# Low halves of the gate and value weights by an adding transfer from GpSimd instead of a VectorE subtraction

## The chip, the core and the metric

The kernel runs on one core of a Trainium2 chip. The metric is the device time of one execution in microseconds, lower is better. Five engines of the core work beside each other, each through its own instructions in their order: TensorE (PE, with its weight loads PEld), VectorE (DVE), ScalarE (ACT), GpSimd (POOL) and SyncE (SP), which here only issues transfers. They wait for each other through semaphores.

## What is computed

```python
def reference(**kwargs):
    attn_out = _attn_ref(**attn_kwargs)                     # q, k, v: (4, 8, 576, 64)
    x = np.ascontiguousarray(attn_out.transpose(0, 2, 1, 3)).reshape(B * S, H * D)
    x = _moe_ref(x=x, **moe_kwargs)                         # 512 -> 1536 -> 512
    return _moe2_ref(x=x, **moe2_kwargs)                    # 512 -> 2048 -> 512

def _attn_ref(q, k, v):
    scores = scale * np.matmul(q, k.transpose(0, 1, 3, 2))
    mask = (rel >= 0) & (rel < 128)
    scores = np.where(mask, scores + bias[None], -1000000000.0)
    attn = softmax of scores along the keys
    return np.matmul(attn, v)

def _moe_ref(x, w_gate, w_val, w_out):
    g = x @ w_gate
    silu = g * (1.0 / (1.0 + np.exp(-g)))
    val = x @ w_val
    return silu * val @ w_out
```

The weights reach the chip as 64-bit floats. Windowed attention with a linear bias makes 2304 tokens of 512 numbers; a gated layer (gate and value weights, then an output weight) and a second layer follow.

## The kernel before, in words

**Split operands.** Matmuls of the two layers run on operands rounded to a shorter 32-bit format (fp32r). To keep accuracy every operand is a pair, a high half (the rounded value) and a low half (the value minus its high half), and a product is three matmuls: high by high, high by low, low by high (`hid`, `proj`, `products`).

**Five chunks of tokens.** The 2304 tokens go through attention and the first layer in chunks of 512, 384, 512, 512 and 384. While PE does the first layer of one chunk, the attention of the next is woven between its groups. Chunk 0 of the first layer is the place that the change touches: a group is one block i of 128 hidden columns (i = 0 to 11). Its gate product is `g()` (12 matmuls of 512 columns), its value product `v()` (12 more), and its part of the output product `o()` (12). The text calls them g5, v5, o5 and so on. Each needs the weight tile w5, a tile of two halves, `h[:, 0]` and `h[:, 1]`.

**Weights made on the way.** `stage_w1` has SP load a raw tile of 64-bit numbers (`wst`, 1 MB). `convert` makes a 32-bit float of it in five steps: one on ACT (L421, into `cg`), four on DVE (L426, L433, L438, L444). L433 is the first that writes the 32-bit tile `cw`, L444 the last. `halves` then has ACT round it into the high half (`hi_act`, L121) and DVE subtract that from it into the low half (`lo_dve`, L124). The same five steps and `halves` make the tiles of the output weight (`conv_ring`, tile `ring`); these are also written to DRAM from `cw`.

**What sets the order.** PE's order is written out by hand. The conversions are a queue of small steps (`bg`) which `pump` takes from between the groups of PE's order, in chunk 0 so that the steps of w(i+2) are handed out about while group i is handed out. On the other engines the scheduler of the framework orders the instructions by its own estimate of when they are ready, so each of DVE, ACT and POOL has a fixed order when the program runs, and an instruction that waits holds up what is behind it on its engine.

**Buffers.** `cw` has two buffers, which the conversions of w, those of `ring` and, at the end of a chunk, the evacuation share. Weight tiles and raw tiles share a pool of 12 (`wp`). The PSUM banks of the scores, the transposed probabilities, the attention output and the gate and value products rotate through four (`rot`): a bank comes free when DVE or ACT has read it.

**POOL** only clears small tiles (`memset`, L204) and masks the transposed probabilities (`affine_select`, L268 and L272, six to a head in chunk 1); the attention output `o_ps` waits for the masks. All transfers are issued by SP.

Of the kernel before, what the change touches and what calls it, by code (L numbers as in the profile page):

```python
# [9 lines left out]
F32 = mybir.dt.float32  # L10
# [5 lines left out]
AF = mybir.ActivationFunctionType  # L16
ALU = mybir.AluOpType
# [75 lines left out]
def body(ctx: ExitStack, tc: tile.TileContext, qT, kT, vP, w1, w1o, w2, cst, yT):  # L93
    nc = tc.nc
# [25 lines left out]
    def hi_act(out, in_):  # L120
        return nc.scalar.activation(out=out, in_=in_, func=AF.Copy)  # L121

    def lo_dve(out, in_, hi):
        return nc.vector.tensor_tensor(out=out, in0=in_, in1=hi.bitcast(F32), op=ALU.subtract)  # L124
# [282 lines left out]
    def steps(key, fs, front=False):  # L407
        if front:
            bg.extendleft([(key if f is fs[-1] else None, f) for f in fs][::-1])
            return  # L410
        for f in fs[:-1]:
            bg.append((None, f))
        bg.append((key, fs[-1]))

    def convert(raw, st):
        words = raw.rearrange("p (n t) -> p n t", t=2)
        top16 = raw.bitcast(BF16).rearrange("p (n t) -> p n t", t=4)[:, :, 3]

        def f1():
            st["g"] = bpool["a"].tile([128, 1024], BF16, tag="cg", name="cg", bufs=2)  # L420
            nc.scalar.activation(out=st["g"], in_=top16, func=AF.Prelu, scale=2.0 ** -112, alpha=-(2.0 ** 32))  # L421

        def f2():
            st["p"] = bpool["a"].tile([128, 1024], BF16, tag="cp", name="cp", bufs=1)
            g, p = st["g"].bitcast(I32), st["p"].bitcast(I32)
            nc.vector.tensor_scalar(  # L426
                out=p, in0=g, scalar1=3, scalar2=-0x007F0080, op0=ALU.logical_shift_left, op1=ALU.bitwise_and
            )

        def f3():  # L430
            st["w"] = hp_.tile([128, 1024], F32, tag="cw", name="cw")
            a = st["w"].bitcast(I32)
            nc.vector.tensor_scalar(  # L433
                out=a, in0=words[:, :, 1], scalar1=0xFFFFF, scalar2=0x100000, op0=ALU.bitwise_and, op1=ALU.bitwise_or
            )

        def f4():
            nc.vector.scalar_tensor_tensor(  # L438
                out=st["w"], in0=words[:, :, 0].bitcast(U32), scalar=2.0 ** -32, in1=st["w"].bitcast(I32),
                op0=ALU.mult, op1=ALU.add,  # L440
            )

        def f5():
            nc.vector.scalar_tensor_tensor(  # L444
                out=st["w"], in0=st["w"], scalar=2.0 ** -20, in1=st["p"], op0=ALU.mult, op1=ALU.mult
            )

        return [f1, f2, f3, f4, f5]

    def halves(st, alloc, put):  # L450
        def f1():
            st["h"] = alloc()
            hi_act(st["h"][:, 0], st["w"])

        def f2():
            lo_dve(st["h"][:, 1], st["w"], st["h"][:, 0])
            put(st["h"])

        return [f1, f2]

    def w_tile():
        return wp.tile([128, 2, 1024], F32R, tag="w", name="w")

# [3 lines left out]
    stage = {}  # L467

    def stage_w1(i):
        stage[i] = wp.tile([128, 2048], I32, tag="w", name="wst")  # L470
        nc.sync.dma_start(out=stage[i], in_=w1[i].bitcast(I32))
# [5 lines left out]
    def conv_w1(i):  # L477
        st = {}

        def put(w):  # L480
            wt[i] = w
            stage.pop(i)
            if i + 4 < NF1:
                stage_w1(i + 4)

        steps(("w", i), convert(stage[i], st) + halves(st, w_tile, put))

    def conv_ring(r):
        st = {}
# [442 lines left out]
    with tc.manual_schedule(engines={mybir.EngineType.PE}):  # L932
# [28 lines left out]
        while at < lasts[0]:  # L961
            pieces.popleft()[2]()
            at += 1
            if at == 1:
                conv_w1(0)
                conv_ring(0)
                conv_w1(1)
                nst = len(bg)
                stage_w1(2)
                stage_w1(3)  # L970
            f = (at / lasts[0] - CFG["conv_a"]) / (CFG["conv_b"] - CFG["conv_a"])
            while bg and nst - len(bg) < f * nst:
                pump(1)
        carry = []
        behind += [last_of["act"], last_of["x", 2]]
        for ci, p in enumerate(plansA):
# [33 lines left out]
            for gi, (kind, i, f) in enumerate(groups):  # L1010
                if ci == 0 and kind == "gv" and gi % 3 == 0:
                    if i + 2 < NF1:
                        conv_w1(i + 2)
                    if i == 0:
                        conv_ring(1)
                f()
                if ci or not win:
                    pump(CFG["pump_g"])
                elif gi % 3 == 0:
                    due = max(1, -(-len(bg) // 4))  # L1020
                if not ci:
                    pump(due)
                while win and (spent * ng < (gi + 1) * total or gi == len(groups) - 1):
                    _, cost, e = win.popleft()
                    e()
                    spent += cost
                    pump(CFG["pump_p"] if ci else due)
# [76 lines left out]
```

## Time and profile before

| | |
|---|---|
| device time, median of 3 runs | 962.4 us (958.83 to 965.27) |
| device time of the profiled execution | 964.91 us |
| its span in the trace | 963.2 us |
| PE busy | 927.9 us (96%) |
| DVE busy | 699.3 us (73%) |
| ACT busy | 526.1 us (55%) |
| POOL busy | 213.8 us (22%) |

All rows come from one profiled execution; times in them are microseconds from the start of the span. Busy time is the time in which an engine worked on instructions. In a timeline a row stands for one or more like instructions, xN is their number, and the bracket at its end is the idle time of the engine ahead of it with the instruction that ended it. PEclk is the clock that TensorE was granted, as a share of 2.4 GHz, so that 0.50 is the lower level of 1.2 GHz.

### The profile page before, as it was taken

What the parts mean: (1) busy time and instruction counts of PE and PEld (TensorE: products, weight loads), DVE (VectorE), ACT (ScalarE), POOL (GpSimd) and SP (SyncE); (2) the same over time, 40 slices, a digit from 0 to 9 for tenths busy, and PEclk for the clock granted to TensorE, in tenths of its full rate; (3) what the DMA queues carried; (4) which work ended last, traced back from release to release, by engine and by line L of the source; (5) the groups of instructions that cost most, each with busy time, mean ns of one, the idle gap of its engine ahead of it and who ended that gap; (6) DMA issues with size and microseconds to landing.
All of it is one profiled execution on the core that took longest, in us unless ns stands there. A gap on an engine that the chain in (4) does not pass through costs nothing. (4 is left out here: it accounts for less than half of the span.)

```text
span 963.2 us, 14607 instructions
## 1 busy us (share of the span) xinstructions
PE 927.9 (96%) x5040; PEld 831.0 (86%) x5040; DVE 699.3 (73%) x1341; ACT 526.1 (55%) x1135; POOL 213.8 (22%) x332
## 2 busy tenths in 40 slices
PE   6999989999999999998999998899999999999998
PEld 4757777899988888886878998889999999999998
DVE  6789998688767855477434668778876888777673
ACT  6757676666575764445433445555544645454442
POOL 0217422101211122001113334552012320122000
PEclk9979999999999999999999999999999999999999
DMA  8736536377537632276306993624784257830375
GB/s 304 284 110 249 176 103 195 92 243 264 161 86 246 220 115 94 73 233 212 113 1 215 378 325 109 251 66 156 259 296 141 66 180 250 309 116 21 95 259 193
DMA packets 76921, 174.86 MB, mean 182 GB/s; under 512 B 9136, under 2 KB 52528, under 8 KB 67120
## 3 DMA queue, kind: packets, MB, share of 16 engines
q1 hardware_dynamic: 76848, 173.94, 54.3%
q8 instruction: 40, 0.66, 0.3%
q14 instruction: 33, 0.27, 0.1%
HBM read 138.25 MB, written 35.65 MB: 181 GB/s over the span
## 5 line engine op out<-in xcount | busy, mean ns | idle before, releaser
L114 PE MATMUL g_ps<-xt,w 128*128 128x512 f32 (+1 forms) x1440 | 320.6, 376 | 1.3 <-ACT xt L121 0.7
L114 PEld LDWEIGHTS g_ps<-xt,w 128*128 128x128 f32 x1440 | 260.0, 190 | 38.9 <-issue 2.4
L114 PE MATMUL bk<-xs,win 128*128 128x384 f32 x1008 | 179.0, 336 | 8.0 <-DVE G L699 6.0
L114 PEld LDWEIGHTS bk<-xs,win 128*128 128x128 f32 x1008 | 174.4, 188 | 12.2 <-DVE G L699 9.6
L114 PE MATMUL bk<-op,wout 128*128 128x384 f32 x1008 | 175.6, 334 | 0.4 <-DMA wout<-w2o 0.4
L114 PEld LDWEIGHTS bk<-op,wout 128*128 128x128 f32 x1008 | 174.8, 188 | 0.7 <-issue 0.7
L114 PE MATMUL acc<-hh,ring 128*128 128x512 f32 (+1 forms) x480 | 150.2, 376 | 2.3 <-DVE ring L124 1.6
L268 POOL TENSOR_SCALAR_AFFINE_SELECT PT<-PT 128x256 f32<-128x256 f32 (+4 forms) x80 | 55.5, 710 | 247.5 <-ACT PT L265 247.4
L121 ACT ACTIVATE op<-G 128x768 fp32r<-128x768 f32 x84 | 70.7, 846 | 65.6 <-PE bk L114 63.1
L114 PEld LDWEIGHTS acc<-hh,ring 128*128 128x128 f32 x480 | 89.8, 190 | 16.0 <-DVE ring L124 2.3
L124 DVE TENSOR_TENSOR op<-G,op 128x768 fp32r<-128x768 f32 x84 | 80.1, 960 | 26.9 <-ACT op L121 26.4
L795 POOL TENSOR_TENSOR t<-w 128x256 f32<-128x256 f32 x48 | 44.4, 945 | 224.6 <-DVE win L124 205.8
L114 PE MATMUL acc<-hl,ring 128*128 128x512 f32 (+1 forms) x240 | 89.2, 372 | 0.8 <-DVE hl L124 0.8
L237 ACT ACTIVATE Pt<-Pt,sm 128x128 f32<-128x128 f32 (+1 forms) x160 | 62.4, 392 | 20.5 <-DVE sm L233 20.1
L634 DVE SCALAR_TENSOR_TENSOR t<-t,g_ps 128x512 f32<-128x512 f32 (+1 forms) x60 | 37.6, 627 | 37.6 <-ACT t L633 37.5
L633 ACT ACTIVATE t<-g_ps 128x512 f32<-128x512 f32 (+1 forms) x60 | 32.8, 546 | 53.1 <-PE g_ps L114 52.6
L699 DVE TENSOR_TENSOR G<-u,bk 128x384 f32<-128x384 f32 x72 | 38.9, 552 | 31.4 <-PE bk L114 29.3
L1048 ACT ACTIVATE G<-G 128x384 f32<-128x384 f32 x72 | 36.9, 519 | 44.2 <-DVE G L699 44.2
L642 DVE SCALAR_TENSOR_TENSOR t<-t,g_ps 128x512 f32<-128x512 f32 (+1 forms) x60 | 37.8, 630 | 28.4 <-PE g_ps L114 27.4
L121 ACT ACTIVATE hh<-t 128x512 fp32r<-128x512 f32 (+1 forms) x60 | 35.0, 583 | 40.5 <-DVE t L642 40.4
L252 ACT ACTIVATE Pt<-Pt,sm 128x128 f32<-128x128 f32 (+1 forms) x144 | 46.3, 391 | 12.2 <-DVE sm L248 12.1
L114 PEld LDWEIGHTS acc<-hl,ring 128*128 128x128 f32 x240 | 45.5, 190 | 6.3 <-DVE hl L124 1.1
(78 smaller groups left out, 1241.0 us busy)
## 6 DMA issues: line engine op xcount, KB each, us to landing
wout<-w2o SPq DMA_DIRECT2D x42, 1024.0 KB, 5.8
wraw<-w SPq DMA_DIRECT2D x16, 1024.0 KB, 5.9
w2o<-chl SPq DMA_DIRECT2D x16, 896.0 KB, 8.3
wst<-w SPq DMA_DIRECT2D x12, 1024.0 KB, 7.2
cw<-w1od SPq DMA_DIRECT2D x24, 512.0 KB, 4.0
w<-w2d SPq DMA_DIRECT2D x24, 512.0 KB, 3.4
w2d<-cw SPq DMA_DIRECT2D x16, 512.0 KB, 4.3
wraw<-w1o SPq DMA_DIRECT2D x6, 1024.0 KB, 5.1
```

Of the source, the lines that this page charges most:

```text
L114: nc.tensor.matmul(out=out, lhsT=lhsT, rhs=rhs, start=start, stop=stop, skip_group_check=True)
L121: return nc.scalar.activation(out=out, in_=in_, func=AF.Copy)
L124: return nc.vector.tensor_tensor(out=out, in0=in_, in1=hi.bitcast(F32), op=ALU.subtract)
L237: nc.scalar.activation(out=Pt[:q.qn], in_=Pt[:q.qn], func=AF.Exp, scale=-1.0, bias=sm[:q.qn, i:i + 1], accum_out=sm[:q.qn, 8 + i:9 + i],)
L252: nc.scalar.activation(out=pt, in_=pt, func=AF.Copy, scale=r)
L268: nc.gpsimd.affine_select(out=here, in_=prev, pattern=[[0, m], [1, n]], compare_op=ALU.is_ge, fill=0.0, base=0, channel_multiplier=-1,)
L633: tanhs.append(nc.scalar.activation(out=t[:, :n], in_=st["g"][:, :n], func=AF.Tanh, scale=0.5))
L634: nc.vector.scalar_tensor_tensor(out=t[:, :n], in0=t[:, :n], scalar=1.0, in1=st["g"][:, :n], op0=ALU.add, op1=ALU.mult)
L642: nc.vector.scalar_tensor_tensor(out=t[:, :n], in0=t[:, :n], scalar=0.5, in1=vps[:, :n], op0=ALU.mult, op1=ALU.mult)
L699: nc.vector.tensor_tensor(out=out, in0=a, in1=b, op=op)
L795: nc.gpsimd.tensor_tensor(out=x[:, o], in0=a, in1=b, op=ALU.subtract)
L1048: nc.scalar.activation(out=out, in_=in_, func=AF.Mish)
```

## The change

For the weight tiles 2 to 11 the two steps of `halves` are replaced by those of `fold`. ACT rounds the 32-bit tile into the high half as before. Then ACT writes the negated high half into the place of the low half, and a transfer issued by GpSimd adds the 32-bit tile onto it. The tiles 0 and 1, all `ring` tiles and the second layer's weights keep the subtraction on DVE.

```diff
@@ -458,6 +458,19 @@
+    def fold(st, put):
+        def f1():
+            st["h"] = w_tile()
+            hi_act(st["h"][:, 0], st["w"])
+
+        def f2():
+            h = st["h"]
+            nc.scalar.activation(out=h[:, 1], in_=h[:, 0].bitcast(F32), func=AF.Copy, scale=-1.0)
+            nc.gpsimd.dma_start(out=h[:, 1].bitcast(F32), in_=st["w"], accum_op=ALU.add)
+            put(h)
+
+        return [f1, f2]
+
@@ -483,7 +496,7 @@
-        steps(("w", i), convert(stage[i], st) + halves(st, w_tile, put))
+        steps(("w", i), convert(stage[i], st) + (fold(st, put) if i > 1 else halves(st, w_tile, put)))
```

The 13 new lines move every later line: L633 and L642 of before are L646 and L655 after. PE's order stays as it is. On the other engines the scheduler sets a new order, for the stretch in which chunk 0 of the first layer runs and, in a few places, near the end of the chunks. Three places of it follow. The number behind a name tells one buffer's use from the next; in brackets stands which engines or transfers the instruction waits for (DMAHW: a transfer issued by SP, DMASW: one issued by GpSimd).

On DVE, before the change, the stretch in which the first output-weight tile of the woven part (`cw_825`) and w5 (`cw_895`) begin to be converted. `t_820` is the gate of group 3 (L634), `hl_749` the low half of group 2's hidden block.

```order
L124 TENSOR_TENSOR w_788<-cw_771,w_788 128x1024 [waits DMAHW3_49,Activation_49]
L438 SCALAR_TENSOR_TENSOR cw_825<-wraw_643,cw_825 128x1024 [waits DVE_49]
L248 RECIPROCAL sm_664<-sm_664 128x4 [waits DVE_49]
L124 TENSOR_TENSOR hl_749<-t_692,hh_748 128x512 [waits Activation_49]
L226 COPY_PREDICATED s_ps_774<-cst_sb_76,s_ps_774 128x128 [waits PE_49]
L433 TENSOR_SCALAR cw_895<-wst_485 128x1024 [waits DMAHW3_49,DVE_49]
L444 SCALAR_TENSOR_TENSOR cw_825<-cw_825,cp_823 128x1024 [waits DVE_49]
```

And now, the same stretch, where these tiles are `cw_828` and `cw_898`, the gate is `t_823` (L647) and the low half `hl_751`.

```order
L124 TENSOR_TENSOR hl_751<-t_693,hh_750 128x512 [waits Activation_49]
L433 TENSOR_SCALAR cw_828<-wraw_644 128x1024 [waits DMAHW4_49,DMASW1_49]
L438 SCALAR_TENSOR_TENSOR cw_828<-wraw_644,cw_828 128x1024 [waits DVE_49]
L433 TENSOR_SCALAR cw_898<-wst_485 128x1024 [waits DMAHW3_49,DMASW2_49]
L444 SCALAR_TENSOR_TENSOR cw_828<-cw_828,cp_826 128x1024 [waits DVE_49]
L438 SCALAR_TENSOR_TENSOR cw_898<-wst_485,cw_898 128x1024 [waits DVE_49]
L226 COPY_PREDICATED s_ps_830<-cst_sb_76,s_ps_830 64x64 [waits PE_49]
L647 SCALAR_TENSOR_TENSOR t_823<-t_823,g_ps_810 128x512 [waits Activation_49]
```

The subtraction for w4 (`w_788`) is gone from DVE, and the L433 of each new tile, which waited for DVE's own earlier instruction and for a transfer of SP, now waits for an adding transfer: `cw_828` for that of w3, `cw_898` for that of w4. The gate of group 3 stands behind both.

On POOL, before the change, the masks of one head of chunk 1 (`PT_761`).

```order
L204 MEMSET sm_1705 128x8 [waits DVE_49,Activation_49]
L268 AFFINE_SELECT PT_761<-PT_761 128x64 [waits Activation_49]
L272 AFFINE_SELECT PT_761<-PT_761 128x64 [waits Pool_49]
L268 AFFINE_SELECT PT_761<-PT_761 128x2x128 [waits Activation_49]
L268 AFFINE_SELECT PT_761<-PT_761 128x64 [waits Activation_49]
L272 AFFINE_SELECT PT_761<-PT_761 128x2x128 [waits Pool_49]
L272 AFFINE_SELECT PT_761<-PT_761 128x64 [waits Pool_49]
```

And now, the same head's masks (`PT_763`), with the issues of the adding transfers for w3 (`w_697`) and w4 (`w_790`).

```order
L469 DMA w_697<-cw_677 128x1024 [waits DMAHW2_49,DMAHW1_49,DMAHW6_49,DMAHW0_49,DMAHW7_49,DVE_49,Activation_49]
L268 AFFINE_SELECT PT_763<-PT_763 128x64 [waits Activation_49]
L268 AFFINE_SELECT PT_763<-PT_763 128x2x128 [waits Activation_49]
L272 AFFINE_SELECT PT_763<-PT_763 128x64 [waits Pool_49]
L268 AFFINE_SELECT PT_763<-PT_763 128x64 [waits Activation_49]
L272 AFFINE_SELECT PT_763<-PT_763 128x2x128 [waits Pool_49]
L272 AFFINE_SELECT PT_763<-PT_763 128x64 [waits Pool_49]
L469 DMA w_790<-cw_773 128x1024 [waits DMAHW4_49,DMAHW5_49,DMAHW3_49,DMAHW6_49,DVE_49,Activation_49]
```

The transfer for w3 is issued ahead of the head's six masks and that for w4 behind them; the next one (w5) stands behind the six masks of the head after it.

On ACT, before the change, from the rounding of w4 (`w_788`) on.

```order
L121 ACTIVATE w_788<-cw_771 128x1024 [waits DVE_49]
L265 ACTIVATE PT_761<-t_ps_756 128x64 [waits PE_49,Pool_49]
L121 ACTIVATE hh_748<-t_692 128x512 [waits DVE_49]
L265 ACTIVATE PT_761<-t_ps_756 128x2x128
L265 ACTIVATE PT_761<-t_ps_756 128x64
L421 ACTIVATE cg_966<-wst_599 128x1024 [waits DMAHW5_49,DVE_49]
```

And now, from the rounding of w4 (`w_790`, first row) to its negation (last row).

```order
L121 ACTIVATE w_790<-cw_773 128x1024 [waits DVE_49]
L421 ACTIVATE cg_970<-wst_600 128x1024 [waits DMAHW5_49,DVE_49]
L265 ACTIVATE PT_763<-t_ps_758 128x64 [waits PE_49,Pool_49]
L265 ACTIVATE PT_763<-t_ps_758 128x2x128
L265 ACTIVATE PT_763<-t_ps_758 128x64
L121 ACTIVATE hh_750<-t_693 128x512 [waits DVE_49]
L468 ACTIVATE w_790<-w_790 128x1024 [waits Activation_49]
```

Five other instructions stand between the rounding and the negation of w4.

## Rows read from the trace of the kernel before

**Rows 1.** The page, busy time of each engine, share of the span, instructions.

```profile
PE 927.9 (96%) x5040; PEld 831.0 (86%) x5040; DVE 699.3 (73%) x1341; ACT 526.1 (55%) x1135; POOL 213.8 (22%) x332
```

**Rows 2.** Busy time by stretch; columns: length, each engine's busy time, PEclk, DMA share, GB/s.

```profile
75.00:100.00 25.00, 24.79 (x108) 17.96 (x107) 25.00 (x46) 19.03 (x48) 18.69 (x15) 1.00 0.72 265
100.00:125.00 25.00, 21.81 (x115) 17.16 (x114) 24.88 (x55) 16.38 (x42) 13.56 (x13) 0.98 0.50 161
125.00:150.00 25.00, 23.89 (x125) 18.95 (x124) 24.64 (x54) 17.34 (x46) 6.43 (x14) 0.95 0.43 132
...
125.00:127.50 2.50, 2.50 (x8) 1.88 (x7) 2.50 (x5) 2.30 (x6) 0.00 (x0) 0.54 0.64 225
```

**Rows 3.** Timeline of PE in chunk 0; columns: start, length, engine, line, operation, tiles.

```profile
91.79 0.48 PE L114 MATMUL s_ps<-k,q 64*128 64x256 f32 x1
...
92.88 5.77 PE L114 MATMUL g_ps<-xt,w 128*128 128x512 f32 x24
...
103.66 5.77 PE L114 MATMUL g_ps<-xt,w 128*128 128x512 f32 x24
...
119.78 0.70 PE L259 MATMUL t_ps<-cst_sb,Pt 128*128 128x128 f32 x4 [0.57 <-DVE t L634]
123.10 0.36 PE L114 MATMUL s_ps<-K,Q 128*128 128x256 f32 x1 [2.62 <-ACT Pt L237]
...
123.58 0.42 PE L114 MATMUL acc<-hh,ring 128*128 128x512 f32 x1
...
127.95 0.25 PE L114 MATMUL s_ps<-K,Q 128*64 128x192 f32 x1
...
135.36 0.39 PE L114 MATMUL acc<-hh,ring 128*128 128x512 f32 x1
...
138.10 0.64 PE L259 MATMUL t_ps<-cst_sb,Pt 128*128 128x128 f32 x4
...
146.92 0.38 PE L114 MATMUL s_ps<-K,Q 128*128 128x256 f32 x1 [1.11 <-DVE Q L193]
```

**Rows 4.** Instructions on the weight tiles: number, ns least/median/most, first and last start.

```profile
L121 ACT ACTIVATE w<-cw x12: 1039/1056/1072, 18.7 to 151.4; 128x1024 fp32r<-128x1024 f32 x12
L124 DVE TENSOR_TENSOR w<-cw,w x12: 1182/1210/1385, 21.5 to 153.8; 128x1024 fp32r<-128x1024 f32 x12
```

**Rows 5.** Timeline of ACT: the rounding of w4.

```profile
77.86 1.04 ACT L121 ACTIVATE w<-cw 128x1024 fp32r<-128x1024 f32 x1
```

**Rows 6.** Timeline of DVE around the conversions of w4 and w5.

```profile
82.36 0.67 DVE L433 TENSOR_SCALAR cw<-wst 128x1024 int32<-128x1024 int32 x1
...
89.53 1.23 DVE L124 TENSOR_TENSOR w<-cw,w 128x1024 fp32r<-128x1024 f32 x1
...
91.09 0.68 DVE L634 SCALAR_TENSOR_TENSOR t<-t,g_ps 128x512 f32<-128x512 f32 x1
91.69 1.21 DVE L438 SCALAR_TENSOR_TENSOR cw<-wst,cw 128x1024 f32<-128x1024 uint32 x1
```

**Rows 7.** Timeline of POOL: first and last masks of two heads.

```profile
79.07 6.80 POOL L268 TENSOR_SCALAR_AFFINE_SELECT PT<-PT 128x64 f32<-128x64 f32 x1 [0.96 <-ACT PT L265]
...
91.17 2.43 POOL L272 TENSOR_SCALAR_AFFINE_SELECT PT<-PT 128x256 f32<-128x256 f32 x2
...
121.57 0.59 POOL L268 TENSOR_SCALAR_AFFINE_SELECT PT<-PT 128x64 f32<-128x64 f32 x2
...
122.50 1.36 POOL L272 TENSOR_SCALAR_AFFINE_SELECT PT<-PT 128x256 f32<-128x256 f32 x2
```

**Rows 8.** Transfers: tiles, queue, number, KB each, median us from issue to landing.

```profile
wst<-w SPq DMA_DIRECT2D x12, 1024.0 KB, 7.2
cw<-w1od SPq DMA_DIRECT2D x24, 512.0 KB, 4.0
w<-w2d SPq DMA_DIRECT2D x24, 512.0 KB, 3.4
...
v<-vP SPq DMA_DIRECT2D x32, 32.0 KB, 2.1
```

## Prediction

> **What bounds the kernel now.** I read the page first, then busy time by stretch, then the timelines of PE, DVE, ACT and POOL where the stretches pointed, then the transfers. The page has PE busy for 927.9 us (96%) and DVE for 73% [rows 1], so over the whole program DVE looks free. The stretch in which the changed conversions run does not look like that: from 75 to 150 us DVE is busy for 25.00, 24.88 and 24.64 of each 25 us, while PE is busy for 24.79, 21.81 and 23.89 [rows 2]. Here DVE is full and PE sometimes waits for it. Outside of this stretch nothing that the change touches stands near PE's path, so the forecast is a sum over it.
>
> The reader should see in PE's timeline how little there is to win. PE stands idle for 0.57 us until DVE has made a gate (L634), 2.62 us until ACT has made an exponential, and 1.11 us until DVE has made a query tile (L193): 4.30 us [rows 3]. After the longest of these the granted clock falls: 0.54 in the stretch from 125.0 to 127.5 [rows 2], where about 1.0 is 2.4 GHz and 0.5 is 1.2 GHz. The twelve matmuls of one output group take 123.58 to 127.95, that is 4.37 us, and the same twelve 135.36 to 138.10, 2.74 us at full clock [rows 3]. That is 1.63 us more. A DVE with more room can give back at most 4.30 + 1.63 = 5.93 us, whatever is taken off it.
>
> **The change part by part.** *Removed:* ten subtractions of 1.210 us on DVE, 12.1 us [rows 4]. Their worth on the path is bounded by 0 and 5.93 us. The two waits for DVE itself (0.57 + 1.11 = 1.68) I count as gone; the wait put to ACT and the slow clock behind it (2.62 + 1.63 = 4.25) I count at half, since ACT's exponential follows work of DVE but also stands in ACT's queue. Gain: 1.68 + 2.12 = 3.8 us.
>
> *Added on ACT:* ten negations. They have the size of the rounding, 1.056 us [rows 4], 10.6 us together. ACT is idle for 5.97, 8.62 and 7.66 us of the three stretches [rows 2], 22.3 us, which hides them as load. Were that cover gone they would cost up to 10.6 us. They do lengthen the way from the 32-bit tile to the finished weight, which is counted next.
>
> *Added: the adding transfer.* No row shows one, and none shows a transfer issued by GpSimd. The rows bound its way from issue to landing by 2.1 us (32 KB) and 7.2 us (1 MB); plain transfers of its 512 KB take 3.4 and 4.0 [rows 8]. It has to read both what it adds and what it adds to, 1 MB in all, so I take a value nearer to the 1 MB row: 6.0 us. The Trainium skill, "DMA: Bandwidth & Descriptors", section on the anatomy of one DMA on the SWDGE (gpsimd) path, fits plain transfers of GpSimd by 2.0 us plus the bytes at 436 GB/s, by its figures an estimate of 3.2 us here. With that in place of 6.0 the sum below would be that of the first rival; no run here shows it yet.
>
> *Moved: who waits for whom.* Before, the buffer `cw` was free again when DVE itself had subtracted. Now it is free when the transfer has landed, and the next conversion's first step on DVE (L433) waits for that, with everything behind it in DVE's order. With two buffers, w5 waits for w4's transfer. I follow these two.
>
> *First place, w4.* Its rounding starts at 77.86 [rows 5] and ends at 78.90. In the new order five ACT instructions stand between it and the negation; I put them at 3.0 us, an estimate from the 1.06 us of one of that size and about half for the smaller ones. With the negation, 83.0. POOL has six masks ahead of the issue. Such a head's masks took from 79.07 to 93.60, 14.5 us, and another's from 121.57 to 123.86, 2.3 us [rows 7]. The slow ones ran while DVE was busy for all of the stretch [rows 2]. I take 2.3, as DVE will be waiting here itself, and part of it passes beside ACT's work: issue at 84, landing at 90. Group 4 wants w4 at 92.88 [rows 3], so PE does not wait for the weight. But DVE's L433 of w5, which ran at 82.36 [rows 6], now waits to 90. Between it and the gate of group 3 stand 0.67 + 1.21 + 1.21 us of conversion and a short copy of 0.2, 3.3 us in all, so the gate starts at 93.3 instead of 91.09 [rows 6]. The scores at 91.79 [rows 3] take the bank that this gate frees, with nothing to spare. PE loses 2.2 us.
>
> *Second place, w5.* Behind the gate (0.68) DVE has some 4.2 us of work up to the end of w5's L444: to 98.2. Rounding and negation, 2.1 us: 100.3. The masks of the next head are ahead on POOL, 2.3 us: issue at 102.6 to 103, landing at 109. Before, w5 was finished at 90.76 [rows 6], 12.9 us ahead of its use at 103.66 [rows 3]. PE, already 2.2 us late, would want it at 105.9 and waits 3.1 us. A wait of that length was followed by the lower clock before, so 1.6 us come on top.
>
> *Later weights.* w7 and w9 wait for the transfers of w6 and w8 in the same way. Each can cost between 0 and w5's 3.1 us; I take 1.0 each, 2.0.
>
> *Sum:* 2.2 + 3.1 + 1.6 + 2.0 - 3.8 = +5.1 us. Against the profiled execution's own 964.91 us (963.2 of span and 1.7 around it) that is 970.0. This execution lies 2.5 us above the median of 962.4, so the forecast is 967.5 us.
>
> **The rivals.** *First: the transfers are quick and DVE keeps its gain.* If an adding transfer lands as a plain one of 512 KB does, 3.4 to 4.0 us [rows 8], w4 lands at 87.5 to 88, the gate of group 3 starts near its old time, w5 lands by 104.5, and every wait of PE above goes: 962.4 - 5.9 = 956.5 us. The rows of plain transfers speak for it, the doubled reading and POOL's queue against it. It decides from a landing of less than about 4 us. A gain of more than 1% would need even more: the slow clock elsewhere to go too.
>
> *Second, on the other side: POOL is starved.* If the masks ahead of w4's issue run as slowly as those from 79.07, the first of which took 6.80 us while two others took 0.59 together [rows 7], w4 is issued at 93.6 and lands at 99.6. The gate of group 3 then comes at 102.9, w5's L444 ends at 107.8, its negation at 109.9, its issue at 112.2, its landing at 118.2: 14.5 us behind the old start of group 5. With the lower clock twice (3.3) and the gain of 3.8 taken off: +14.0, 976.4 us. It decides once the masks ahead of an issue take more than about 6 us. The rows show both speeds, the slow one where DVE is full; against it speaks that a DVE that waits is not full. The Trainium skill, "SBUF — State Buffer", section "SBUF: two separate sides", has a rule on this: while DVE runs an instruction in its two-port mode GpSimd is locked out of the port pair they share and cannot write descriptors for its transfers. By that rule the issues themselves, not only the masks, would be late, and the time would be this rival's. The masks' two speeds agree with the lock; no run here shows an issue.
>
> *Third: nothing comes of it.* DVE waits for about the 12.1 us that it was relieved of, in places where PE does not follow, or the waits and gains cancel: 962.4 us, give or take 2.
>
> **How the numbers follow.** A measurement of this kernel tells about 1% from no change, 9.6 us: below 952.8 or above 972.0. The forecast gets 0.35 (its own range 962.5 to 972.5; 0.30 within 1%, 0.05 slower), the quick transfers 0.22 (0.17 within, 0.05 faster), the starved POOL 0.33 (0.02 within, 0.31 slower), no effect 0.10 (within). Together 0.05 faster, 0.59 within 1%, 0.36 slower. The range goes from the full gain to a little beyond the starved POOL: 956 to 980.
>
> **What would show it right or wrong.** Right: DVE idle ahead of L433 of w5 and of later tiles, released by a transfer of GpSimd, 3 to 7 us each; adding transfers with 5 to 7 us from issue to landing; an idle PE near group 5 that ends with the weight. DVE's busy time should fall by 12 us and ACT's rise by 10.6. Wrong on the fast side: landings of 4 us or less, no idle time of DVE ahead of L433, PE's waits of 4.30 us gone. Wrong on the slow side: issues that stand on POOL behind masks of several us, PE idle for more than 5 us at one group. If the waits lie elsewhere (the ring tiles, the scores' banks), the mechanism is another than this one.

## Result, and the profile after

The changed kernel takes 970.55 us (median of 5 runs, 968.41 to 971.43), the kernel before beside it 964.24 us (5 runs, 958.83 to 965.27). The ratio is 1.0084, 95% interval 1.0061 to 1.0107: slower by 0.84%, 8.1 us (the two medians lie 6.3 us apart), within the 1% named in the prediction. The profiled execution took 970.55 us with a span of 968.8, 5.6 us more than the span before.

The page first, as in [rows 1].

```profile
PE 927.8 (96%) x5040; PEld 830.4 (86%) x5040; DVE 691.6 (71%) x1331; ACT 533.9 (55%) x1145; POOL 200.4 (21%) x342
```

DVE lost ten instructions and 7.7 us, ACT gained ten and 7.8 us, and POOL, which got ten instructions more, is busy for 13.4 us less. The prediction wanted 12 us less of DVE and 10.6 more of ACT: the signs are right, the sizes smaller. PE's work is the same to 0.1 us, in a span that is 5.6 us longer: what was lost is waiting. Busy time by stretch says where (columns as in [rows 2], whose first two stretches answer to the last two).

```profile
50.00:75.00 25.00, 19.01 (x72) 11.21 (x71) 21.84 (x46) 15.86 (x32) 4.62 (x6) 0.86 0.41 127
75.00:100.00 25.00, 21.99 (x92) 16.07 (x91) 15.83 (x35) 14.56 (x35) 4.92 (x14) 0.93 0.88 274
100.00:125.00 25.00, 25.00 (x129) 19.63 (x128) 21.30 (x45) 18.08 (x40) 8.60 (x13) 1.00 0.58 155
```

From 75 to 100 us DVE has fallen from 25.00 to 15.83, 9.2 us, where the three subtractions of this stretch took 3.6 before, and PE from 24.79 to 21.99. Both stand still. From 100 to 125 PE has become full. The list of waits of PE up to 250 us names the places:

```profile
PE g_ps L114 <- DMA w<-cw: 7.1, 3, 3.9
...
PE s_ps L114 <- DVE Q L193: 5.1, 3, 1.9
```

(waiting tile, what it waited for: us in total, times, the longest.) A weight finished by an adding transfer, which [rows 3] do not know as a releaser, is now PE's largest. The timeline of PE shows the three waits for it and what follows.

```profile
60.44 1.65 PE L114 MATMUL g_ps<-xt,w 128*128 128x512 f32 x6
...
63.11 0.72 PE L114 MATMUL g_ps<-xt,w 128*128 128x512 f32 x2
67.69 4.63 PE L114 MATMUL g_ps<-xt,w 128*128 128x512 f32 x10 [3.86 <-DMA w<-cw]
...
76.31 2.91 PE L114 MATMUL g_ps<-xt,w 128*128 128x512 f32 x12
...
83.46 0.63 PE L114 MATMUL g_ps<-xt,w 128*128 128x512 f32 x2
87.09 3.93 PE L114 MATMUL g_ps<-xt,w 128*128 128x512 f32 x10 [3.01 <-DMA w<-cw]
...
98.85 5.77 PE L114 MATMUL g_ps<-xt,w 128*128 128x512 f32 x24
...
119.08 2.93 PE L114 MATMUL g_ps<-xt,w 128*128 128x512 f32 x12
...
127.06 0.39 PE L114 MATMUL s_ps<-K,Q 128*128 128x256 f32 x1 [1.39 <-DVE Q L193]
...
130.75 0.69 PE L114 MATMUL g_ps<-xt,w 128*128 128x512 f32 x2
131.65 2.58 PE L114 MATMUL g_ps<-xt,w 128*128 128x512 f32 x10 [0.21 <-DMA w<-cw]
...
150.80 0.38 PE L114 MATMUL s_ps<-K,Q 128*128 128x256 f32 x1 [1.91 <-DVE Q L193]
...
156.04 2.98 PE L114 MATMUL g_ps<-xt,w 128*128 128x512 f32 x12
```

The first two matmuls of a group use only the high half of the weight, which ACT had rounded in time. The third uses the low half, so the wait stands behind x2: 3.86 us for w2, 3.01 for w3, 0.21 for w7. The same groups before, and the starts of g6, g7 and g9 (the x6 of either list are the last six matmuls of v1):

```profile
61.35 2.93 PE L114 MATMUL g_ps<-xt,w 128*128 128x512 f32 x6
...
66.19 4.45 PE L114 MATMUL g_ps<-xt,w 128*128 128x512 f32 x12
...
74.30 2.91 PE L114 MATMUL g_ps<-xt,w 128*128 128x512 f32 x12
...
82.13 2.91 PE L114 MATMUL g_ps<-xt,w 128*128 128x512 f32 x12
...
85.85 3.04 PE L114 MATMUL g_ps<-xt,w 128*128 128x512 f32 x12
...
113.11 2.93 PE L114 MATMUL g_ps<-xt,w 128*128 128x512 f32 x12
...
128.32 2.98 PE L114 MATMUL g_ps<-xt,w 128*128 128x512 f32 x12
...
150.57 2.98 PE L114 MATMUL g_ps<-xt,w 128*128 128x512 f32 x12
```

Comparing starts, after minus before, gives a ledger of PE. v2: +2.0 (76.31 against 74.30). Less than the 3.86 us of the wait, because the kernel before ran g2 at the lower clock (4.45 us for twelve matmuls that take 2.91 later) and the changed one came to it 3.1 us earlier (63.11 against 66.19). These 3.1 us are not the work of the transfers: the last six matmuls of v1 took 2.93 us before and 1.65 after, as the granted clock was 0.50 from 60.0 to 62.5 us in this execution of the kernel before and 1.00 in that of the changed one, and no weight that the change touches is used ahead of g2.

g4: +6.0 (98.85 against 92.88 [rows 3]). Here the wait of 3.01 counts in full, and the lower clock behind it too: g3's gate takes 0.63 + 3.93 = 4.56 us instead of 2.91. With the 3.1 us set aside it would be +9.1, and in e3_neg below, which has no adding transfer and whose clock does not fall there, g4 does start 9.1 us ahead of the changed kernel (89.77).

Then nothing is lost up to g6. From g6 to g7 3.5 us come back: 119.08 to 130.75, 11.7 us, where the kernel before took 15.2 (113.11 to 128.32), since its waits of 0.57 and 2.62 us and the slow clock behind them [rows 3] are gone and one query wait of 1.39 has come. From g7 to g9 3.0 are lost again, 0.5 at g7 and the rest to the query wait of 1.91 (1.11 before [rows 3]) and to the lower clock that now follows it:

```profile
152.50:155.00 2.50, 2.50 (x8) 1.98 (x7) 0.98 (x4) 1.25 (x2) 2.12 (x6) 0.52 0.59 156
```

g9 starts 5.5 us late (156.04 against 150.57), and that is the 5.6 us of the span: the rest of the program adds 0.1. With the 3.1 us of clock set aside these 5.6 become 8.7, close to the 8.1 of the ratio, which rests on five executions of each kernel.

Why the weights were late is read from the transfers. The list of DMA issues has the ten adding transfers at a median of 5.8 us to landing:

```profile
wst<-w SPq DMA_DIRECT2D x12, 1024.0 KB, 7.7
...
w<-cw POOLq DMA_DIRECT2D x10, 512.0 KB, 5.8
```

One by one, from w2 to w11, they took 8.5, 9.6, 7.4, 4.6, 5.0, 10.7, 4.9, 5.4, 5.3 and 6.3 us. They were issued at 59.16, 77.45, 82.23, 102.19, 108.12, 120.87, 131.73, 148.64, 153.80 and 170.19. SP's timeline shows a load of 1 MB just ahead of the longest ones (8.5, 9.6, 10.7); the first and the last of them also had a raw ring tile (1 MB) and a write of 512 KB ahead:

```profile
55.02 0.43 SPq L484 DMA_DIRECT2D wst<-w  x1
...
74.74 0.58 SPq L484 DMA_DIRECT2D wst<-w  x1
76.52 0.59 SPq L484 DMA_DIRECT2D wst<-w  x1
...
119.43 0.72 SPq L484 DMA_DIRECT2D wst<-w  x1
```

DVE waits for the same landings at the first instruction of the next conversions. Its waits from 40 to 200 us:

```profile
DVE cw L433 <- DMA w<-cw: 13.6, 6, 4.7
```

and its timeline where the prediction looked, group 3:

```profile
87.07 0.69 DVE L433 TENSOR_SCALAR cw<-wraw 128x1024 int32<-128x1024 int32 x1 [4.69 <-DMA w<-cw]
...
89.61 0.69 DVE L433 TENSOR_SCALAR cw<-wst 128x1024 int32<-128x1024 int32 x1 [0.58 <-DMA w<-cw]
...
92.62 0.67 DVE L647 SCALAR_TENSOR_TENSOR t<-t,g_ps 128x512 f32<-128x512 f32 x1
```

The raw tile tells which is which: `wraw` is the first ring tile, waiting for w3's landing (77.45 + 9.6), `wst` is w5, waiting for w4's (82.23 + 7.4), and L647 is the gate of group 3. PE does not wait for that gate: at 92 us it is itself some 6 us late.

Last, ACT and POOL: the negations (L468, on the weight tiles) and what stands ahead of w4's issue (L469).

```profile
L468 ACT ACTIVATE w<-w x10: 1044/1062/1072, 57.8 to 168.2; 128x1024 fp32r<-128x1024 f32 x10
...
L469 POOL DMA_DIRECT2D w<-cw x10: 862/884/1037, 59.2 to 170.2; - x10
```

```profile
77.45 0.86 POOL L469 DMA_DIRECT2D w<-cw  x1 [6.33 <-ACT w L468]
80.10 0.67 POOL L268 TENSOR_SCALAR_AFFINE_SELECT PT<-PT 128x64 f32<-128x64 f32 x2 [1.79 <-ACT PT L265]
...
81.11 0.60 POOL L272 TENSOR_SCALAR_AFFINE_SELECT PT<-PT 128x256 f32<-128x256 f32 x2
82.23 0.88 POOL L469 DMA_DIRECT2D w<-cw  x1 [0.53 <-ACT w L468]
```

Six masks took 80.10 to 81.71, 1.6 us, and no issue took more than 1.04 us.

### The profile page after: what moved, and what is told of

It is laid out like the page before. It is cut to its first block, busy times and chain, and to the rows that moved or that the text cites. A ratio compares the mean times of both kernels' runs of the same rounds, so it can differ in the third digit from the quotient of the medians.

```text
span 968.8 us, 14636 instructions
## 1 busy us (share of the span) xinstructions
PE 927.8 (96%) x5040; PEld 830.4 (86%) x5040; DVE 691.6 (71%) x1331; ACT 533.9 (55%) x1145; POOL 200.4 (21%) x342
## 5 line engine op out<-in xcount | busy, mean ns | idle before, releaser
L114 PEld LDWEIGHTS bk<-xs,win 128*128 128x128 f32 x1008 | 174.3, 188 | 11.4 <-DVE G L712 8.9
L268 POOL TENSOR_SCALAR_AFFINE_SELECT PT<-PT 128x256 f32<-128x256 f32 (+4 forms) x80 | 44.4, 570 | 242.4 <-ACT PT L265 242.2
L647 DVE SCALAR_TENSOR_TENSOR t<-t,g_ps 128x512 f32<-128x512 f32 (+1 forms) x60 | 37.7, 628 | 32.3 <-ACT t L646 32.0
L646 ACT ACTIVATE t<-g_ps 128x512 f32<-128x512 f32 (+1 forms) x60 | 32.8, 547 | 46.7 <-PE g_ps L114 46.6
L655 DVE SCALAR_TENSOR_TENSOR t<-t,g_ps 128x512 f32<-128x512 f32 (+1 forms) x60 | 37.8, 631 | 27.6 <-PE g_ps L114 26.6
L124 DVE TENSOR_TENSOR hl<-t,hh 128x512 fp32r<-128x512 f32 (+1 forms) x60 | 40.1, 669 | 15.7 <-ACT hh L121 15.2
```

What stands on the lines that cost most here:

```text
L114: nc.tensor.matmul(out=out, lhsT=lhsT, rhs=rhs, start=start, stop=stop, skip_group_check=True)
L268: nc.gpsimd.affine_select(out=here, in_=prev, pattern=[[0, m], [1, n]], compare_op=ALU.is_ge, fill=0.0, base=0, channel_multiplier=-1,)
L646: tanhs.append(nc.scalar.activation(out=t[:, :n], in_=st["g"][:, :n], func=AF.Tanh, scale=0.5))
L647: nc.vector.scalar_tensor_tensor(out=t[:, :n], in0=t[:, :n], scalar=1.0, in1=st["g"][:, :n], op0=ALU.add, op1=ALU.mult)
L655: nc.vector.scalar_tensor_tensor(out=t[:, :n], in0=t[:, :n], scalar=0.5, in1=vps[:, :n], op0=ALU.mult, op1=ALU.mult)
```

## The experiments

The theory, formed on this profile: the loss is PE's two direct waits for the low halves of w2 and w3, the weights with the least time to spare. Rival B: it is the buffer `cw`, held until the landing, with DVE's gates and queries queued behind the waiting L433. The expectations also name a rival A: that each of the ten transfers pays a like share. Two smaller suspects: the negations on ACT, and the adding itself against the mere sharing of the DMA engines.

**The negation alone (e3_neg).** The low half is made from the negated high half as after, but by DVE.

```diff
-            nc.gpsimd.dma_start(out=h[:, 1].bitcast(F32), in_=st["w"], accum_op=ALU.add)
+            nc.vector.tensor_tensor(out=h[:, 1], in0=st["w"], in1=h[:, 1].bitcast(F32), op=ALU.add)
```

> The ten negations on ScalarE stay, but VectorE adds the 32-bit tile onto them, as many VectorE instructions as in the kernel before, and no transfer is issued by GpSimd. Theory (the loss is the transfer's landing): 1 us below to 3 us above before. Rival A in the form of ScalarE (10.6 us more in its queue delay what TensorE waits for): 4 to 7 us above before.

Measured: 960.87 us against 960.66, ratio 1.0001 (0.9982 to 1.0020). Ten negations on ACT, 10.6 us of busy time, cost nothing; what is lost comes with the transfer. The starts of g4, g6 and g7 in its trace serve as a second kernel without transfers:

```profile
89.77 5.77 PE L114 MATMUL g_ps<-xt,w 128*128 128x512 f32 x24
...
110.00 2.93 PE L114 MATMUL g_ps<-xt,w 128*128 128x512 f32 x12
...
120.89 2.98 PE L114 MATMUL g_ps<-xt,w 128*128 128x512 f32 x12
```

**Without w2 and w3 (e1_late).** Only w4 to w11 get their low half from the transfer.

```diff
-        steps(("w", i), convert(stage[i], st) + (fold(st, put) if i > 1 else halves(st, w_tile, put)))
+        steps(("w", i), convert(stage[i], st) + (fold(st, put) if i > 3 else halves(st, w_tile, put)))
```

> Only w4 to w11 get the adding transfer; w2 and w3 keep the subtraction on VectorE. Theory (the loss is the way of w2 and w3 through the transfer, whose landing comes after TensorE wants them: waits of 3.86 and 3.01 us, and the lower clock behind them; the later eight have room): no wait of TensorE at groups 2 and 3, group 4 starts near 93 us as before, the time is 4 us below to 1 us above before. Rival A (each of the ten pays a like share, through ScalarE's ten negations or GpSimd's queue): eight tenths of the loss stay, 4 to 6 us above before. Rival B (the waits of VectorE for the two cw buffers make the loss): six of those waits are of w4 and later, so at least 3 us above before.

Measured: 976.26 against 960.66, ratio 1.0155 (1.0134 to 1.0176). With two transfers fewer it is slower still: the theory falls as the whole explanation, and so does a like share for each transfer. The timeline of DVE:

```profile
91.87 0.69 DVE L433 TENSOR_SCALAR cw<-wst 128x1024 int32<-128x1024 int32 x1 [9.65 <-DMA w<-cw]
...
95.49 0.67 DVE L647 SCALAR_TENSOR_TENSOR t<-t,g_ps 128x512 f32<-128x512 f32 x1
...
130.99 0.69 DVE L433 TENSOR_SCALAR cw<-wraw 128x1024 int32<-128x1024 int32 x1 [5.67 <-DMA w<-cw]
...
134.65 0.56 DVE L193 SCALAR_TENSOR_TENSOR Q<-qraw,Q 64x384 fp32r<-64x384 f32 x1
```

and that of PE:

```profile
96.21 2.05 PE L114 MATMUL s_ps<-k,q 64*128 64x256 f32 x4 [5.20 <-DVE t L647]
...
99.00 7.77 PE L114 MATMUL g_ps<-xt,w 128*128 128x512 f32 x24 [0.74 <-DVE sm L233]
...
135.26 0.58 PE L114 MATMUL s_ps<-K,Q 128*128 128x256 f32 x1 [7.45 <-DVE Q L193]
```

This is the chain the prediction described for w4: the transfer issued at 83.24 lands 8.6 us later, w5's L433 waits for it for 9.65 us, the gate of group 3 stands behind, and PE's scores wait 5.20 us for the gate. At 131 us it repeats with a query tile behind the waiting L433, 7.45 us of PE. (The 7.77 us of g4, against 5.77 [rows 3], are the lower clock after the wait.) So what B names can cost PE more than the direct waits do, where these do not come first.

**Only w2 and w3 (e2_first).**

```diff
+        steps(("w", i), convert(stage[i], st) + (fold(st, put) if 1 < i < 4 else halves(st, w_tile, put)))
```

> Only w2 and w3 get the adding transfer; w4 to w11 keep the subtraction on VectorE. Theory: the whole loss stays, waits of TensorE of 3 to 4 us at groups 2 and 3, 6 to 9 us above before (the gain later on, the waits of before near 120 us, is not had). Rival A: two tenths of the loss, 1 to 2 us above before. Rival B: two of the waits for the buffers, 1 to 3 us above before.

Measured: 971.53 against 960.66, ratio 1.0118 (1.0087 to 1.0148). Waits from 40 to 250 us:

```profile
PE g_ps L114 <- DMA w<-cw: 7.2, 2, 4.5
...
DVE cw L433 <- DMA w<-cw: 1.4, 2, 1.2
```

With the direct waits (landings 9.2 and 9.3 us) and hardly a wait of DVE, 10.9 us are lost by the medians, more than the 6 to 9 expected. Both mechanisms show in the traces, and their costs do not add: 10.9 for w2 and w3, 15.6 for w4 to w11, 6.3 by the medians for all ten. A likely reason is that a PE which is 6 us late at g4 no longer feels a gate that is late by less; how much each kernel's own order has to do with it is not shown.

**Only the last five (e10_last5),** `i > 6`.

> The adding transfer for w7 to w11 only, the weights with the most room before their use, with the two buffers. If VectorE's relief of 1.2 us a weight is worth anything where it is full (the waits of 4.30 us and the slow clock of 1.63 near 120 us): 0 to 5 us below before. Theory (VectorE's first conversion step waits for a landing with gates behind it, and gives back more than it gains): 1 to 8 us above before.

Measured: 969.95 against 961.99, ratio 1.0080 (1.0053 to 1.0107): half of the transfers cost as much as all. DVE waits once for 4.34 us, and PE behind it 4.18 us for a query tile; and once for 8.81 us, at a landing of 11.2 us with two SP transfers (`wraw`, `w1od`) issued less than a microsecond ahead. No subset of the weights tried here is free.

**Adding against copying (e4_plain).** The transfer copies the 32-bit tile into the low half; the adding is left out, so the low halves hold the whole weight.

```diff
-            nc.gpsimd.dma_start(out=h[:, 1].bitcast(F32), in_=st["w"], accum_op=ALU.add)
+            nc.gpsimd.dma_start(out=h[:, 1].bitcast(F32), in_=st["w"])
```

> The transfer stays but copies in place of adding, so the low halves hold the whole 32-bit value: the subtraction is left out. If reading its destination makes the transfer long, the landing falls from 5.8 us in the middle to 3.5 to 4.5, the waits of TensorE at groups 2 and 3 fall by half or more and 3 us or more of the loss are had back. If the share of the transfer engines with SyncE's raw loads of 1 MB makes it long (8.5 and 9.6 us where such loads were issued just before, 4.6 where not), the landings for w2 and w3 stay above 7 us, and the time stays within 2 us of the changed kernel's.

Measured: 964.39 (10 runs, 957.28 to 969.03 and one of 973.78, which the ratio leaves out) against 960.66, ratio 1.0022 (0.9994 to 1.0050). Its instructions on POOL, and PE's wait for weights up to 250 us:

```profile
L469 POOL DMA_DIRECT2D w<-cw x10: 527/546/822, 58.7 to 168.0; - x10
```

```profile
PE g_ps L114 <- DMA w<-cw: 4.0, 2, 2.7
```

Landings are 2.9 to 9.1 us, median 4.8, against 4.6 to 10.7 and 5.8 with the adding; the issue takes 0.55 us of POOL instead of 0.88. Nine of the ten weights land 1.2 to 2.7 us sooner (w8 later, 9.1 against 4.9), and PE's waits fall from 7.1 to 4.0 us. The time comes back to within 0.5% of before, so most of the loss goes with the adding, as the first half of the expectation has it. But the copies for w2 and w3 still take 7.3 and 8.0 us, and others up to 9.1, as the second half has it: the adding alone does not make the landings long. How much of the time that came back is owed to the shorter landings and how much to this kernel's own order is not shown.

**A landing without a load beside it (e8_hold).** The raw load that is issued when a weight is done waits until that weight's adding transfer has landed.

```diff
+            st["x"] = nc.gpsimd.dma_start(out=h[:, 1].bitcast(F32), in_=st["w"], accum_op=ALU.add)
...
+                x = stage_w1(i + 4)
+                if "x" in st:
+                    landed = mybir.DependencyInfo(mybir.DependencyClass.Sync, mybir.DependencyReason.DATA)
+                    tc.add_manual_dep(x.ins, st["x"].ins.name, landed, reason="landed")
```

> The changed kernel, but SyncE's raw loads for w6 to w11 each wait until the adding transfer of the weight four before has landed. In the changed kernel adding transfers landed after 8.5, 9.6, 7.4 and 10.7 us where 1 MB loads had been issued up to 4 us before, and after 4.6 to 6.3 us elsewhere. Theory (they share the transfer engines with these loads): w3 and w4 land within 6 us, TensorE's wait for w3 (3.01 us) goes, that for w2 (its neighbour, the load for w5, is not held) stays; 3 to 6 us above before. If the adding itself, or GpSimd's writing of descriptors beside a busy VectorE, made them long: landings for w3 and w4 of 7 us or more stay, and the time stays within 2 us of the changed kernel's 8 above before.

Measured: 980.4 (972.87 to 987.03) against 961.99, ratio 1.0185 (1.0117 to 1.0253). The landing of w2 fell from 8.5 to 5.2 us and that of w3 from 9.6 to 4.6; PE's wait for w2 is gone, and that for w3 fell to 1.9. The expectation had the neighbour of w2 wrong: the load issued ahead of it is that for w6, the seventh, which was held. So the load does lengthen the transfer. The landing of w4 rose, though, from 7.4 to 9.0 us, with a raw ring tile and a write of 512 KB issued 2.4 and 1.2 us ahead. The time is worse:

```profile
PE g_ps L114 <- DMA w<-cw: 10.6, 5, 4.0
```

Five weights (w3, w4, w8, w9, w11) miss their groups, by 10.6 us in all; w3 and w4 are issued at 80.5 and 89.6 us instead of 77.5 and 82.2. From 40 to 250 us the trace shows no conversion on ACT or DVE that waits for a held load, so that these loads come too late is not what it shows; what delays the five stays open.

**The same for w4 to w11 (e9_hold_late).**

> As e8_hold, with the adding transfer for w4 to w11 only (as in e1_late, 15 us above before, where w4 landed after 8.6 us and VectorE waited 9.65 us for it). Theory (the landing is shared with loads, and VectorE waits for it): w4 lands within 6 us, VectorE's longest wait for a landing falls below 6 us, and the time falls to 3 to 10 us above before. If it is the order that counts: 12 us or more above before stay.

Measured: 973.35 against 961.99, ratio 1.0113 (1.0075 to 1.0150), where e1_late has 1.0155; their intervals just touch. w4 lands after 5.4 us instead of 8.6, and DVE's longest wait is 6.49 instead of 9.65 us. A landing 3.2 us shorter is a wait 3.2 us shorter. The time, 11.4 us above before, lies between the two expectations.

**A third buffer (e5_third, e6_late_third, e7_before_third).** The odd weights are converted in a 32-bit buffer of their own: in the kernel after, in e1_late, and, as a control, in the kernel before, which has no transfer to wait for.

```diff
+            if own:
+                st["w"] = bpool["a"].tile([128, 1024], F32, tag="cwa", name="cwa", bufs=1)
+            else:
+                st["w"] = hp_.tile([128, 1024], F32, tag="cw", name="cw")
```

> The kernel before with the third 32-bit buffer for the odd w3 to w11, to see what the buffer alone does. Theory: VectorE is full there and never waits for a buffer, so nothing: within 2 us of before. If the buffer by itself frees the order: 3 us or more below before, and then e5_third and e6_late_third are to be read against this run.

> Adding transfers for w4 to w11 only, with the third 32-bit buffer for the odd w5 to w11. Theory (with the two late weights left out, what made e1_late 15 us slower is VectorE waiting 9.65 and 5.67 us for a landing with gates and query tiles behind it): these waits go, TensorE's waits of 5.20 and 7.45 us with them, and the time is 5 us below to 3 us above before. If the scheduler's new order as such made e1_late slow: 8 us or more above before stay.

> The changed kernel with a third 32-bit buffer, which the odd w3 to w11 use, so that the landing of one transfer holds up fewer of the next conversions. Theory (two causes, the late landing for TensorE at groups 2 and 3, and VectorE's first conversion step waiting for the landing): the first stays, with waits of TensorE for w2 and w3 of 5 to 8 us in all, the second falls, VectorE's waits for an adding transfer go from 13.6 us to under 6: 4 to 8 us above before. If the waits for the buffer alone made the loss of the changed kernel: within 2 us of before.

Measured against 963.26: the control 969.36, ratio 1.0056 (1.0039 to 1.0074); with w4 to w11 on transfers 970.09, 1.0086 (1.0056 to 1.0117); with all ten 974.24, 1.0121 (1.0106 to 1.0136). The control was not neutral: a buffer that no one needs costs some 5 us. With it DVE and ACT get another order, and g4 starts at 101.76 instead of 92.88 [rows 3]. Read against it, the transfers of w4 to w11 cost 0.7 us where they cost 15.6 with two buffers, and the waits of 5.20 and 7.45 us do not occur; that supports B. With w2 and w3 as well 4.9 us remain. No wait of PE for a weight over 0.9 us shows there, so this rest is not shown to be the direct waits, and DVE still waits four times for a landing, 13.1 us in all, where under 6 were expected. Against the kernel before all three expectations missed.

None of these kernels is faster than the one before; e3_neg equals it.

## Why the prediction was right or wrong

**The sum.** +5.1 us was forecast against the profiled execution; 5.6 us were found between the two, 8.1 by the ratio. The time of 970.55 us lies in the range of 956 to 980 and 3 us above the forecast of 967.5, and the sign is right. The parts are partly others, and the closeness of +5.1 to 5.6 is luck: 3.1 us of lower clock in the profiled execution of the kernel before hide as much of the loss.

**Landing: right in the middle, wrong in the spread.** "I take a value nearer to the 1 MB row: 6.0 us" measured 5.8 as a median. One value stood for all ten, though, and the two that decided took 8.5 and 9.6 us, beside loads of 1 MB. The Trainium skill, "DMA: Bandwidth & Descriptors", section on the anatomy of one DMA on the SWDGE (gpsimd) path, gives an estimate of 3.2 us for a plain transfer of this size by its figures. The plain ones of e4_plain took 2.9 to 5.0 us where no load of 1 MB was issued shortly ahead, so trace and page roughly agree for an undisturbed copy, and not for an adding or a disturbed one.

**The step that failed: "With two buffers, w5 waits for w4's transfer. I follow these two."** I followed the first weight at which DVE would be held, and never put w2 and w3, which are changed too, beside their groups. Both have less time to spare than w4 (the third matmul of g2 would have run at about 63.8, and w2 landed at 67.7), and PE waited for them directly, 3.86 and 3.01 us, with the lower clock behind each (1.65 us at g3). On the ledger that is the whole +6.0 at g4, 9.1 without the clock of the kernel before. The stretch of the sum began too late for it as well ("Outside of this stretch nothing that the change touches stands near PE's path", from 75 us on): the first transfer was issued at 59.16, and PE waited for it up to 67.69.

**First place, w4: right as a mechanism, hidden in this kernel.** Landing forecast at 90, measured 89.6; gate of group 3 forecast at 93.3, measured at 92.62. The larger wait stood one tile earlier, at the ring tile that waits for w3 (4.69 us). The 2.2 us of PE were not lost, as PE was then later than the gate; e1_late, where it was not, lost 5.20 there.

**Second place, w5: did not occur.** Issue forecast at 102.6 to 103 and landing at 109; measured 102.19 and 106.8, 2.8 us ahead of a g5 that had itself moved to 109.63. The 3.1 + 1.6 us of this term fell at w3 instead, in nearly the same size (3.01 + 1.65), which is why the sum held. That is partly luck.

**Later weights.** 1.0 us each for w7 and w9 was to come from waits for w6's and w8's transfers. PE waited 0.21 us for w7 and nothing for w9; but a query wait of 1.91 us and the lower clock after it took most of the 3.0 us lost between g7 and g9. Another of 1.39 stands ahead of g7.

**The gain: right in size, not shown in cause.** 3.8 us were counted, 3.5 came back from g6 to g7. The parts are others: the waits of 0.57 and 2.62 and the slow clock went wholly (4.82), a wait of 1.39 came, and the query wait of 1.11, counted as gone, grew to 1.91. Nor is it shown that DVE's relief brought it. From g6 to g7 e3_neg, in which DVE has as many instructions as before, takes 10.9 us, less than the 11.7 of the changed kernel, and e2_first, with two subtractions fewer, 13.5, where the kernel before took 15.2. The new order, or a PE that comes later, can do the same.

**ACT hides the negations: right,** by e3_neg.

**Rivals.** The quick transfers fall: no landing is under 4.6 us. The starved POOL falls too: issues of 0.86 to 1.04 us and masks of 1.6 us. The Trainium skill, "SBUF — State Buffer", section "SBUF: two separate sides", whose lock spoke for it, isn't contradicted, since DVE stood still for 4.69 us just there, but no issue in this case was held up by it for long enough to be seen.

**Still open.** Each kernel also has its own scheduled order, and e7_before_third shows that a new order alone can be worth 5 us. How much of the differences between e1_late, e2_first and e10_last5 is order and how much is transfers isn't settled; DVE's order wasn't pinned by hand. For the change itself the ledger rests on waits whose releaser is the transfer, and that part doesn't depend on it. What the later part of the ledger owes to the order, the gain above all, is open.

## What to carry to other kernels

Moving work from a full engine to a transfer trades 1.2 us of engine time for 4.6 to 10.7 us of latency here, on the result and on the source buffer, so each consumer has to be checked for slack, the first ones ahead of all, and each next writer of the buffer for what is queued behind it on its engine. Price a transfer for the moment in which it runs, with the loads issued just ahead of it, not by a median. And where a scheduler sets the order, run the neutral edit (here the unused buffer) as a control before reading a difference of half a per cent as an effect.

## What the runs showed of the hardware that I had not expected

A 1 MB load issued up to 4 us ahead can nearly double the way of a 512 KB adding transfer: 8.5, 9.6 and 10.7 us in the changed kernel, each with a second 1 MB load close by, against 4.6 to 6.3 in the other places (7.4 beside another adding transfer), and 5.2 for w2 once the load for w6 was held back. With one such load and otherwise smaller ones beside it a transfer took 9.2 and 9.7 us where the load was issued 0.2 and 0.7 us ahead (e10_last5, e1_late), and 6.2 and 6.9 where it was 1.7 and 2.0 us (e9_hold_late, e8_hold).

An adding transfer holds POOL for 0.88 us at its issue and a plain one for 0.55, for the same tiles.

POOL's masks (L268) went from 55.5 us of busy time to 44.4, though none was removed: an engine's busy time can fall because of what another one does. That DVE was full does not explain the long masks by itself: before, the six masks from 121.57 us took 2.3 us while DVE was busy for 2.23 of 2.29, the first four of them beside short instructions of the softmax, and the one of 6.80 us ran mainly beside conversions. Which of DVE's instructions hold a mask up wasn't tested.
